# Masks on quarter tiles, K in four loads, early zero products and two tiles' K from memory, in a fused attention and mixture kernel

## The chip, the cores and the metric

The kernel runs on one core of a Trainium2 chip. The metric is the device time in microseconds of one execution. A profiled execution has a time of its own and a span, from its first to its last instruction. The engines are TensorE (PE, with its weight loads as PEld), VectorE (DVE), ScalarE (ACT), GpSimd (POOL) and SyncE (SP), whose queue issues all loads and stores here.

## What is computed

The reference chains three blocks. An attention with a window of 16 positions to each side and 24 block summaries, for 2 batches of 8 heads with 768 positions of 64 numbers; a feed-forward block with a Mish-like gate; a soft mixture of 8 experts with 4 slots each. Cut to what matters here:

```python
k_sum = k.reshape(B, H, nb, block, D).max(axis=3)
scores_l = scale * np.matmul(q, k.transpose(0, 1, 3, 2))
mask_l = np.abs(pos[:, None] - pos[None, :]) < window
scores_s = scale * np.einsum('bhsd,bhnd->bhsn', q, k_sum) + np.log(block)
scores_all = np.concatenate([np.where(mask_l, scores_l, -1e9), scores_s], axis=-1)
a = softmax(scores_all)
x = np.matmul(a, np.concatenate([v, v_sum], axis=2))   # 1536 tokens of 512
h = x @ w_in                                          # 512 to 2048
g = h * np.tanh(np.log1p(np.exp(h)))
x = g @ w_out                                         # then the soft mixture of experts
```

## The kernel before, in words

The 1536 tokens are 12 tiles of 128, six for each batch. Attention of a tile `t` handles two windows of 64 queries, with 96 neighbouring keys and 24 summaries each (KW = 120 columns). Its score step (`S`, L410 to L420) is 32 products on quarters of the PE array (64 rows by 64 columns, `tile_position`), four heads' pairs into two banks of 480 columns. For the first five tiles the mask is added by PE: a product of `spread_sb` (an identity over both halves, and three rows of ones) with a block of `mask_sb`, started ahead of the scores in the same bank (L414). It has the mask's 96 columns in rows 0 to 63 and the summand log(32) in rows 64 to 66 of columns 96 to 119. Later tiles get the mask on VectorE from a block made once (`near_mask`, `edge_mask`).

K of the first batch is loaded whole (`ld_kb`, L314, two loads of 768 KB), VectorE takes the block maxima (`ksum`, L319), and GpSimd copies the summaries (`kplace`, L372) and each tile's window (`windows`, L360) into the tile's K block. Tiles 0 to 5 all take their windows from there; tiles 8 to 11 load theirs from memory (`ld_k`, L401). After the scores come the row maximum (`red`, L427), its negative (`neg`, L431), exponentials on ScalarE (`exp`, L441), the reciprocal of the sums (`rc`), the scaling (`nm`, L456, on GpSimd or VectorE), the transposes (`AT`, L462) and the product with V (`AV`, L472).

Beside this the weights are prepared: `w_in` comes packed in eight loads (`ld_wi`, L496) through three staging slots, and each is decoded by ScalarE (`dec_a`, L487) and VectorE (`dec_s`, L488; `dec_o`, L489), which frees its slot for the next load. A scale per block is found (`gram`, `sc_bt`), and two half-precision planes are made (`wi_hi`, `wi_lo`, L519). Tile 0 goes through the first feed-forward product in full precision (`H32`, L611), later tiles by three plane products each (`H`, L617 to L619). `w_out` follows in the same way (`ld_wo`), with a folded matrix from it (`W2mm`, L570). Then each tile is routed (`route`), and the experts' weights stream in through whatever slots are free.

Every piece of work is a task. `ORDER` lists all 1281 of them in the order in which they are written to their engines' queues, `CHOICE` gives the engine of those that may run on several, and `SLOT` the buffer of each. So an engine does its tasks in the order of that table, and waits where one's inputs are late. The DMA queue has eight completion lanes: the ninth load of the program waits for the first to have landed, the tenth for the second, and so on.

## Time and profile before

| | us |
|---|---|
| median of 3 runs (lowest, highest) | 290.21 (289.18, 291.86) |
| profiled execution, its own time | 289.33 |
| its span | 287.5 |
| outside the span | 1.83 |
| busy in the span: PE, DVE, ACT, POOL | 268.0, 195.0, 207.8, 52.2 |

Busy times of PE are modelled ends, so a stretch that shows PE fully busy can hold slow products too. The granted clock is a share of PE's full rate (2.4 GHz), 0.5 of it being 1.2 GHz.

### The profile page before, as it was taken

The numbers are of one execution on the slowest core, as the hardware profiler recorded it, in microseconds if no ns is written. First come the engines' busy times: TensorE is split into PE (matmuls) and PEld (weight loads), VectorE is DVE, ScalarE is ACT, GpSimd is POOL, SyncE is SP. The second block draws the span as 40 slices with busy tenths as digits, with TensorE's granted clock in tenths as the row PEclk, the third lists the DMA queues.
The fourth block names the chain that finished last, engine by engine and source line by source line (L and its number), as shares of the span: only waits on it lengthen the run. The fifth ranks groups of instructions, "written<-read, shape, count | busy, mean of one in ns | idle before, by whom it ended". The sixth has DMA issues, their size and how long they took to land.

```text
span 287.5 us, 7828 instructions
## 1 busy us (share of the span) xinstructions
PE 268.0 (93%) x3144; PEld 151.4 (53%) x3144; DVE 195.0 (68%) x460; ACT 207.8 (72%) x488; POOL 52.2 (18%) x91
## 2 busy tenths in 40 slices
PE   0889879999999999999999999999999998999997
PEld 0557445555456564565556545455645743234475
DVE  2489899999999898778659667686523575002352
ACT  1297889979988879999969999899459653003232
POOL 1559225430070531001211111000000010100000
PEclk9997999999999999999999999999999999999999
DMA  7999999599999879999695677989988999999997
GB/s 253 415 358 344 358 339 365 137 335 308 317 246 315 154 107 222 205 241 223 241 192 128 76 222 141 299 157 210 325 317 313 370 388 314 412 423 421 423 346 252
DMA packets 58467, 80.58 MB, mean 280 GB/s; under 512 B 44352, under 2 KB 47936, under 8 KB 53824
## 3 DMA queue, kind: packets, MB, share of 16 engines
q1 hardware_dynamic: 58432, 80.10, 91.3%
q8 instruction: 24, 0.39, 0.5%
q14 instruction: 11, 0.09, 0.1%
HBM read 66.46 MB, written 3.15 MB: 242 GB/s over the span
## 4 chain that ended last, share of the span: by engine, by line
PE 44%; DVE 20%; DMA 16%; ACT 14%; issue 5%; POOL 1%; SPq 0%; DVEq 0%; ACTq 0%; POOLq 0%
PE bank L617 8%; PE bank L619 7%; PE bank L618 7%; DMA slot<-w2b 6%; DVE slot L489 4%; ACT slot L441 4%; DMA slot<-w2a 3%; PE bank L754 2%; ACT slot L625 2%; DMA slot<-kb 2%; DMA slot<-wi 2%; PE bank L472 2%; DVE slot L488 2%; DMA slot<-wo 2%; ACT L625 2%
## 5 line engine op out<-in xcount | busy, mean ns | idle before, releaser
L617 PE MATMUL bank<-slot,slot 128*128 128x512 f16 x176 | 66.9, 380 | 0.7 <-ACT slot L625 0.7
L618 PE MATMUL bank<-slot,slot 128*128 128x512 f16 x176 | 66.7, 379 | 0.0
L619 PE MATMUL bank<-slot,slot 128*128 128x512 f16 x176 | 66.7, 379 | 0.0
L456 POOL TENSOR_TENSOR slot<-slot,sm 128x480 f32<-128x480 f32 x19 | 22.7, 1197 | 91.7 <-DVE sm L452 25.2
L625 ACT ACTIVATE slot<-bank,scal 128x512 f32<-128x512 f32 x44 | 29.2, 687 | 9.8 <-PE bank L619 6.7
L641 DVE SCALAR_TENSOR_TENSOR slot<-slot,sc,slot 128x512 f16<-128x512 f32 x40 | 30.6, 774 | 4.3 <-ACT slot L637 4.0
L619 PEld LDWEIGHTS <-slot 128*128 128x128 f16 x176 | 17.2, 98 | 21.0 <-DVE slot L480 0.3
L255 ACT COPY slot<-bank 120x512 f32<-120x512 f32 (+5 forms) x45 | 17.7, 430 | 14.3 <-PE bank L923 8.3
L617 PEld LDWEIGHTS <-slot 128*128 128x128 f16 x176 | 17.4, 99 | 16.8 <-issue 0.6
L625 ACT ACT_TABLE_LOAD x20 | 25.7, 1283 | 0.8 <-PE bank L619 0.4
L618 PEld LDWEIGHTS <-slot 128*128 128x128 f16 x176 | 17.2, 98 | 16.6 <-issue 1.5
L441 ACT ACTIVATE slot<-slot,sm 128x120 f32<-128x120 f32 x56 | 21.3, 383 | 0.6 <-DVE sm L435 0.5
L441 ACT ACTIVATE slot<-bank,sm 128x120 f32<-128x120 f32 x40 | 13.9, 369 | 10.5 <-POOL sm L431 10.5
L257 DVE COPY slot<-bank 128x256 f32<-128x256 f32 (+3 forms) x30 | 14.4, 513 | 9.8 <-PE bank L462 4.0
L489 DVE SCALAR_TENSOR_TENSOR slot<-slot,slot 128x1024 int32<-128x1024 int32 x16 | 20.4, 1277 | 0.3
L487 ACT ACTIVATE slot<-slot 128x1024 f32<-128x1024 f32 x16 | 18.6, 1172 | 1.8 <-DMA slot<-wi 1.4
L462 PE MATMUL bank<-ident_sb,slot 128*120 128x128 f32 x96 | 14.7, 278 | 2.1 <-POOL slot L456 1.3
L360 POOL COPY slot<-slot 128x192 f32<-128x192 f32 x26 | 13.8, 550 | 12.4 <-DMA slot<-kb 12.3
L967 PE MATMUL bank<-slot,slot 128*32 128x384 f32 (+1 forms) x256 | 15.2, 382 | 0.2 <-DMA slot<-w2b 0.2
L611 PE MATMUL bank<-slot,slot 128*128 128x512 f32 x32 | 15.4, 599 | 0.0
L472 PE MATMUL bank<-slot,slot 120*64 120x64 f32 x384 | 14.6, 233 | 0.5 <-ACT phi_sb L385 0.3
L419 PE MATMUL bank<-slot,slot 64*64 64x120 f32 x384 | 14.2, 289 | 0.6 <-POOL slot L372 0.6
(175 smaller groups left out, 478.4 us busy)
## 6 DMA issues: line engine op xcount, KB each, us to landing
slot<-w SPq DMA_DIRECT2D x16, 1024.0 KB, 5.5
slot<-w2a SPq DMA_DIRECT2D x12, 960.0 KB, 9.0
slot<-wi SPq DMA_DIRECT2D x8, 1024.0 KB, 6.8
slot<-wo SPq DMA_DIRECT2D x8, 1024.0 KB, 6.0
slot<-vh SPq DMA_DIRECT2D x12, 384.0 KB, 5.3
slot<-w2b SPq DMA_DIRECT2D x4, 1024.0 KB, 18.6
slot<-kb SPq DMA_DIRECT2D x4, 768.0 KB, 5.5
slot<-qh SPq DMA_DIRECT2D x12, 256.0 KB, 5.4
```

The source lines that it names most:

```text
L255: sca.copy(dst, src)
L441: sca.activation(A_b[ha.slot][:, hp], src, AF.Exp, bias=m[:, hp:hp + 1], scale=1.0 if late else 0.125, accum_out=m[:, 4 + hp:5 + hp])
L456: (pool if e == "POOL" else vec).tensor_tensor(A_b[ha.slot], A_b[ha.slot], sm_t[hq.slot][:, 4:8].unsqueeze(2).to_broadcast([128, 4, KW]), ...
L472: pe.matmul(banks[hm.slot][64 * r:64 * r + 64, 128 * hp + 64 * w:128 * hp + 64 * w + 64], Vb[i][:, w, c:c + 64], AT_b[hat2[r].slot][0:KW, ...
L487: d = add("ACT", ("dec_a%d" % n,) + name, lambda e: sca.activation(dst(), st(1).bitcast(F32), AF.Prelu, scale=2.0 ** -112, alpha=-(2.0 ** ...
L489: return add("DVE", ("dec_o%d" % n,) + name, lambda e: vec.scalar_tensor_tensor(di(), st(0), 29, di(), op0=ALU.logical_shift_right, op1=AL ...
L611: pe.matmul(banks[hb.slot], xf_b(hx.slot)[:, dc], slots[hw.slot][:, 512 * dc:512 * dc + 512], start=(dc == 0), stop=(dc == 3))
L617: pe.matmul(ps, x[:, 0, dc], w[:, 0, dc], start=(dc == 0), stop=False)
L618: pe.matmul(ps, x[:, 0, dc], w[:, 1, dc], start=False, stop=False)
L619: pe.matmul(ps, x[:, 1, dc], w[:, 0, dc], start=False, stop=(dc == 3))
L625: g_done[t, fb] = [add("ACT", ("mish", t, fb), lambda e, dst=dst, hb=hb, sc=sc: sca.activation(dst(), banks[hb.slot], AF.Mish, scale=sc), ...
L641: d = add("DVE", ("glo", t, fb), lambda e: vec.scalar_tensor_tensor(pv(1), g(), sfb[:, t // TB:t // TB + 1], pv(0), op0=ALU.mult, op1=ALU. ...
```

## The change

- The mask products run on quarters of the array like the scores. `add_mask` writes the 96 mask columns and the 24 summand columns by two products of 64 rows by 64 columns each, once for each quarter, so eight small products stand where two (or, at an edge tile, four) stood. The constants are loaded so that both halves of the partitions hold them: `spread_sb`, `mask_sb` and the new `bias_sb` in two loads each. The two blocks made once for VectorE are built so as well.
- K of the first batch comes in four loads of 384 KB, each with its own block maximum. It lies in slots 4 and 5 rather than 6 and 7, and the full-precision blocks 2 and 3 of `w_in` move to slots 6 and 7.
- 22 products of zeros (`warm`, 128x128 by 480 columns) are added on PE, after GpSimd has zeroed `vsum`. They form a chain, and `vgather` of the first batch waits for the last.
- Tiles 4 and 5 load their K windows from memory, as tiles 8 to 11 do; eight window copies on GpSimd go.
- `ORDER`, `CHOICE` and `SLOT` are new as a whole (1309 tasks).

```diff
 ORDER = [
-    6, 7, 213, 11, 22, 189, 8, 12, 2, 192, 190, 3, 188, 191, 23, 25, 194, 195, 196, 197, 214, 0, 1, 215, 9, 10,
...
-    L_spread = add("DMA", ("ld_spread",), lambda e: dma(out=spread_sb, in_=spread))
-    L_mask = add("DMA", ("ld_mask",), lambda e: dma(out=mask_sb, in_=masks.rearrange("k p n -> p k n")))
+    for w in range(2):
+        L_spread = add("DMA", ("ld_spread", w), lambda e, w=w: dma(out=spread_sb[HALF[w]]..., in_=...), after=[L_spread])
+        L_mask = add("DMA", ("ld_mask", w), lambda e, w=w: dma(out=mask_sb[HALF[w]], in_=masks[:, 0:64].rearrange("k p n -> p k n")), after=[L_mask])
+        L_bias = add("DMA", ("ld_bias", w), lambda e, w=w: dma(out=bias_sb[HALF[w]], in_=masks[0, 64:128, 96:KW]), after=[L_mask])
...
+    def add_mask(ps, r, w, of, stop):
+
+        a, at = ps.shape[1], (64 * r, 64 * w)
+        for stat, mov, cols in ((slice(0, 64), mask_sb[HALF[r], of, 0:96], slice(0, 96)), (slice(64, 128), bias_sb[HALF[r]], slice(96, KW))):
+            pe.matmul(ps[HALF[w], :, cols], spread_sb[HALF[r], stat], mov.unsqueeze(1).to_broadcast([64, a, cols.stop - cols.start]), start=cols.start == 0, stop=stop and cols.start > 0, tile_position=at)
...
+    Z_w = add("POOL", ("fillw",), lambda e: pool.memset(vsum, 0.0))
+    for j in range(22):
+        warm.append(add("PE", ("warm", j), lambda e: pe.matmul(banks[hwarm.slot][:, 0:480], zeros[:, 0:128], zeros[:, 0:480], start=True, stop=True), [warm[-1]], ...))
...
+            for h in range(2):
+                k4.append(add("DMA", ("ld_kq", i, h), lambda e, i=i, h=h: dma(out=slots[hk[i].slot][:, 768 * h:768 * h + 768], in_=kb[b, :, 2 * i + h]), ...))
+                ks.append(add("DVE", ("ksumq", i, h), lambda e, i=i, h=h: vec.tensor_reduce(ksum[:, 2 * i + h], ..., op=ALU.max), [k4[-1]], use=[hk[i]]))
...
         if b == 0:
-            for t in range(2, TB):
-                K_in[t] = windows
+            K_in[2] = K_in[3] = windows
...
-                for rows, of in () if late else [(slice(0, 128), 1)] if kind == 1 else [(slice(0, 64), min(kind, 1)), (slice(64, 128), max(kind, 1))]:
-                    pe.matmul(ps[rows], spread_sb[:, rows], mask_sb[:, of].unsqueeze(1).to_broadcast([128, 4, KW]), start=True, stop=False)
+                for w, of in () if late else [(0, min(kind, 1)), (1, max(kind, 1))]:
+                    add_mask(ps, r, w, of, False)
```

SP's queue at the start, before: the two loads of K (`kb`) are the first, then the constants, one query tile (`qh`), and V's two (`vn`).

```order
L314 DMA slot_78<-kb 128x1536
L314 DMA slot_79<-kb 128x1536
L264 DMA spread_sb<-spread 128x128
L265 DMA mask_sb<-masks 128x3x120
L400 DMA slot_88<-qh 128x512
L262 DMA ident_sb<-ident 128x128
L263 DMA bmean_sb<-bmean 128x144
L316 DMA slot_87<-vn 128x1536
L316 DMA slot_95<-vn 128x1536
L400 DMA slot_89<-qh 128x512
L496 DMA slot_80<-wi 128x2048
```

The same place now.

```order
L268 DMA spread_sb<-spread 64x2x64 x2
L269 DMA mask_sb<-masks 64x3x120
L270 DMA bias_sb<-masks 64x24
L337 DMA slot_76<-kb 128x768 x2
L337 DMA slot_77<-kb 128x768 x2
L269 DMA mask_sb<-masks 64x3x120
L264 DMA ident_sb<-ident 128x128
L265 DMA bmean_sb<-bmean 128x144
L424 DMA slot_88<-qh 128x512
L270 DMA bias_sb<-masks 64x24
L424 DMA slot_89<-qh 128x512
L520 DMA slot_80<-wi 128x2048
```

Four small loads went ahead of K, the second halves of mask and summand stand behind it, and V's loads moved behind the first two of `w_in`.

PE between the first score step (its last row, L419 before) and the second one's masks, before: the edge block (L393) and the block means of V (L328) stand there.

```order
L419 MATMUL bank_65<-slot_90,slot_88 64x120 x2
L393 LDWEIGHTS spread_sb
L393 MATMUL bank_67<-mask_sb,spread_sb 64x120
...
L328 MATMUL bank_68<-slot_87,bmean_sb 24x128 x12
L328 MATMUL bank_68<-slot_95,bmean_sb 24x128 x12
L414 LDWEIGHTS spread_sb
L414 MATMUL bank_66<-mask_sb,spread_sb 128x480
```

The same place now; the pair of L290 stands there 14 times, and six more pairs stand ahead of the first score step.

```order
L443 MATMUL bank_65<-slot_90,slot_88 64x120 x2
L290 LDWEIGHTS vsum
L290 MATMUL bank_61<-vsum 128x480
...
L278 LDWEIGHTS spread_sb
L278 MATMUL bank_66<-mask_sb,spread_sb 64x4x96
L278 LDWEIGHTS spread_sb
L278 MATMUL bank_66<-bias_sb,spread_sb 64x4x24
```

Zero products took the place of the edge block and V's means, which now come after the second score step.

VectorE around the first decode of `w_in` (L488 and L489), before: its first half stands between the two maxima (L427) of tile 1, its second behind them and the scale of V.

```order
L456 TENSOR_TENSOR slot_91<-slot_91,sm_107 128x480
L427 TENSOR_REDUCE sm_108<-bank_66 128x4
L431 TENSOR_SCALAR sm_108<-sm_108 128x4
L488 TENSOR_SCALAR slot_77<-slot_77 128x1024
L427 TENSOR_REDUCE sm_109<-bank_64 128x4
L431 TENSOR_SCALAR sm_109<-sm_109 128x4
L302 TENSOR_REDUCE bnd<-bank_67 128x1
L287 TENSOR_REDUCE sm_110<-bnd 128x1
L489 SCALAR_TENSOR_TENSOR slot_77<-slot_80,slot_77 128x1024
```

The same place now (maxima L451, scaling L480, decode L512 and L513).

```order
L451 TENSOR_REDUCE sm_109<-bank_66 128x4
L480 TENSOR_TENSOR slot_91<-slot_91,sm_108 128x480
L451 TENSOR_REDUCE sm_110<-bank_64 128x4
L512 TENSOR_SCALAR slot_79<-slot_79 128x1024
L513 SCALAR_TENSOR_TENSOR slot_79<-slot_80,slot_79 128x1024
L475 TENSOR_SCALAR sm_109<-sm_109 128x4
L476 RECIPROCAL sm_109<-sm_109 128x4
```

Both halves of the decode now stand behind both maxima of tile 1, so behind the whole second score step.

## Rows read from the trace of the kernel before

**Rows 1.** The page: busy time, share of the span, instructions of each engine.

```profile
PE 268.0 (93%) x3144; PEld 151.4 (53%) x3144; DVE 195.0 (68%) x460; ACT 207.8 (72%) x488; POOL 52.2 (18%) x91
```

**Rows 2.** Windows: stretch, its length, busy times, granted clock, DMA share, GB/s.

```profile
core 0: us, PE busy (x) PEld busy (x) DVE busy (x) ACT busy (x) POOL busy (x), PEclk, DMA share, GB/s
5.00:10.00 5.00, 1.62 (x13) 0.92 (x17) 3.51 (x2) 0.00 (x0) 2.40 (x10) 1.00 1.07 394
...
50.00:55.00 5.00, 5.00 (x26) 2.02 (x25) 4.93 (x8) 5.00 (x13) 1.91 (x1) 1.00 0.72 184
...
60.00:287.50 227.50, 221.34 (x2646) 122.19 (x2644) 147.29 (x366) 164.39 (x384) 24.44 (x38) 1.00 0.92 269
```

**Rows 3.** Windows by stage, the same columns.

```profile
15.50:60.00 44.50, 39.56 (x399) 24.30 (x391) 42.59 (x89) 39.11 (x88) 21.75 (x28) 0.96 0.92 317
60.00:100.00 40.00, 39.36 (x468) 22.34 (x467) 38.61 (x70) 35.98 (x78) 10.03 (x18) 1.00 1.00 275
```

**Rows 4.** Timeline of SP's queue at the start: start, length, load [wait].

```profile
0.74 0.89 SPq L314 DMA_DIRECT2D slot<-kb  x2
1.67 0.42 SPq L264 DMA_DIRECT2D spread_sb<-spread  x1
2.14 0.56 SPq L265 DMA_DIRECT2D mask_sb<-masks  x1
...
4.31 1.29 SPq L316 DMA_DIRECT2D slot<-vn  x2
7.25 0.33 SPq L400 DMA_DIRECT2D slot<-qh  x1
```

**Rows 5.** Timeline of PE in the first score steps.

```profile
7.79 1.01 PE L414 MATMUL bank<-mask_sb,spread_sb 128*64 128x480 bf16 x4 [7.79 <-DMA mask_sb<-masks]
9.39 2.08 PE L419 MATMUL bank<-slot,slot 64*64 64x120 f32 x32 [0.59 <-POOL slot L372]
...
14.45 0.58 PE L414 MATMUL bank<-mask_sb,spread_sb 128*128 128x480 bf16 x2
14.96 1.05 PE L419 MATMUL bank<-slot,slot 64*64 64x120 f32 x32
...
20.90 1.63 PE L419 MATMUL bank<-slot,slot 64*64 64x120 f32 x32
```

**Rows 6.** Windows of one microsecond, the columns of rows 2.

```profile
22.00:23.00 1.00, 1.00 (x22) 0.70 (x16) 0.96 (x2) 0.96 (x6) 0.88 (x1) 0.50 0.94 328
```

**Rows 7.** Timeline of DVE to the end of the first decode.

```profile
7.26 1.75 DVE L319 TENSOR_REDUCE slot<-slot 128x48 f32<-128x1536 f32 x1 [0.22 <-DMA slot<-kb]
...
16.16 0.82 DVE L456 TENSOR_TENSOR slot<-slot,sm 128x480 f32<-128x480 f32 x1
...
16.90 0.64 DVE L427 TENSOR_REDUCE sm<-bank 128x4 f32<-128x480 f32 x1
...
17.66 0.69 DVE L488 TENSOR_SCALAR slot<-slot 128x1024 int32<-128x1024 int32 x1
...
19.71 1.31 DVE L489 SCALAR_TENSOR_TENSOR slot<-slot,slot 128x1024 int32<-128x1024 int32 x1
```

**Rows 8.** Timeline of PE: the fifth tile's step, the folded matrix, the end.

```profile
54.45 0.57 PE L414 MATMUL bank<-mask_sb,spread_sb 128*128 128x480 bf16 x2
...
61.83 1.08 PE L570 MATMUL bank<-slot,phi_sb 128*32 128x128 f32 x32 [0.21 <-DVE slot L489]
...
279.22 0.58 PE L664 MATMUL bank<-mask_sb,spread_sb 128*128 128x480 bf16 x2
...
282.75 3.20 PE L664 MATMUL bank<-mask_sb,spread_sb 128*128 128x480 bf16 x15
```

**Rows 9.** Groups by line on GpSimd: busy, mean ns, idle before.

```profile
L360 POOL COPY slot<-slot 128x192 f32<-128x192 f32 x26 | 13.8, 550 | 12.4 <-DMA slot<-kb 12.3
```

**Rows 10.** DMA issues: count, KB each, median us to landing.

```profile
out<-slot SPq DMA_DIRECT2D x3, 768.0 KB, 4.8
slot<-kh SPq DMA_DIRECT2D x4, 384.0 KB, 4.7
```

More of the change, by code (lines that the diff above doesn't have):

```diff
@@ L271, in const_fill @@
         pool.memset(bnd[:, 0:5], TINY2)
+    Z_w = add("POOL", ("fillw",), lambda e: pool.memset(vsum, 0.0))
+    hwarm = Hold(hring)
+    zeros = vsum.bitcast(BF16)
+    warm = [Z_w]
+    for j in range(22):
+        warm.append(add("PE", ("warm", j), lambda e: pe.matmul(banks[hwarm.slot][:, 0:480], zeros[:, 0:128], zeros[:, 0:480], start=True, stop=True), [warm[-1]], acq=[] if j else [hwarm], use=[hwarm] if j else []))
     Z_c = add("POOL", ("fill",), const_fill)
@@ L338, in batch @@
             V_read.extend([vs] + vm)
-        vc = add("ACT", ("vgather", b), gather, [vs] + old_v, use=[hb])
+        vc = add("ACT", ("vgather", b), gather, [vs] + (old_v or [warm[-1]]), use=[hb])
         if b == 0:
@@ L383, in near_mask, with mm @@
         hm = Hold(mring)
-        q = add("PE", ("near_mm",), lambda e: pe.matmul(banks[hm.slot][:, 0:KW], spread_sb, mask_sb[:, 1], start=True, stop=True), [L_spread, L_mask] + W2_parts, acq=[hm])
+        def mm(e):
+            for w in range(2):
+                add_mask(banks[hm.slot][:, 0:KW].rearrange("p (a k) -> p a k", a=1), 0, w, 1, True)
+        q = add("PE", ("near_m4",), mm, [L_spread, L_mask] + W2_parts, acq=[hm])
         near_done.append(add("ACT", ("near_ev",), lambda e: sca.mul(near, banks[hm.slot][:, 0:KW], 0.125), [q], use=[hm]))
@@ L391, in mm @@
             for n in range(2):
-                for rows, of in ((slice(0, 64), n), (slice(64, 128), n + 1)):
-                    pe.matmul(banks[hm.slot][rows, KW * n:KW * n + KW], spread_sb[:, rows], mask_sb[:, of], start=True, stop=True)
-        q = add("PE", ("edge_mm",), mm, [L_spread, L_mask], acq=[hm])
+                for w in range(2):
+                    add_mask(banks[hm.slot][:, KW * n:KW * n + KW].rearrange("p (a k) -> p a k", a=1), 0, w, n + w, True)
+        q = add("PE", ("edge_m4",), mm, [L_spread, L_mask], acq=[hm])
         edge_done.append(add("ACT", ("edge_ev",), lambda e: sca.mul(edge_t.rearrange("p n k -> p (n k)"), banks[hm.slot][:, 0:2 * KW], 0.125), [q], use=[hm]))
@@ L419, in sc @@
                         pe.matmul(banks[hs2[r].slot][64 * w:64 * w + 64, KW * hp:KW * hp + KW], Qb[i][d, 4 * w + hp], Kb[i][d, :, 4 * w + hp], start=late, stop=(late or hp == 3), tile_position=(64 * r, 64 * w))
[L420 removed]
+        s = add("PE", ("S" + ("" if late else "m4" if kind == 1 else "e4"), t), sc, [lq, *lks, kp[0], kp[1], L_spread, L_mask] + [last_S[0]], acq=hs2)
         last_S[0] = S_t[t] = s
```

30 lines of the change are left out of this document (18 added, 12 removed), and 160 rows, old and new, of tables (CHOICE, ORDER, SLOT).

## The prediction

> **What bounds the kernel now.** I read the busy shares first, then windows, then the timelines of the places that the change touches. PE is busy for 268.0 of 287.5 us [rows 1], so 19.5 us of idle time is all that a better order can win on PE, apart from slow products. By stage the idle time splits so: 8.4 us before 15.5 us (nearly all of it the wait for K and the masks), 4.9 between 15.5 and 60 (44.5 less 39.56), 6.2 after that (227.5 less 221.34) [rows 2, 3]. The reader is to see that the second part has another bound: VectorE is busy for 42.59 of 44.5 us there, and for 38.61 of 40 in the next stretch [rows 3]. It decodes and splits the weights and serves the softmax at once. Until 100 us VectorE has next to no slack, and from 60 us on PE has little either. So time lost at the start is not made up: whatever delays VectorE's first long stretch by one microsecond delays the whole by about one.
>
> The start itself: the first score step waits until 9.39 us, for K's summaries [rows 5], which come out of two block maxima of 1.75 us, the second from 7.26 on when K has landed [rows 7]. Its 32 products take 2.08 us, the second step's 1.05 [rows 5]: PE ran at half speed until about 14 us, though no window before 20 us shows a lowered clock. At 20.90 the same step takes 1.63 us, and there the granted clock does stand at 0.50, that is 1.2 GHz [rows 5, 6].
>
> **The start, part by part.** K now comes behind four small issues. An issue costs 0.42 (spread) to 0.56 us (masks) whole, and 0.33 is the shortest of these rows [rows 4]. Four make 1.3 to 1.9 us; I take 1.8, since a smaller load is not much cheaper to issue in these rows. So K's last quarter lands at 7.26 + 1.8 = 9.06. Its maximum is half of 1.75, 0.87, where the half K cost 1.75: ready at 9.93, and with 0.3 us for GpSimd's copies at 10.2, against 9.39. Behind K on the queue stand the second halves of mask and summand, with 0.45 MB of constants and queries between; at 394 GB/s [rows 2] these take 1.1 us, so they land at 10.2 as well. The summand's second half must also wait for the first quarter of K by the lanes, as the second V load (1.29 us for two issues) and the query load at 7.25 do now [rows 4]; that is over before it matters. Then come four of the mask products in front of the scores, some 0.4 us at half speed. The scores start at 10.6.
>
> Six zero products run ahead of that. A product of 480 columns takes 0.2 us at full speed (15 of them in 3.20, with the last one's end [rows 8]), so 0.4 at half: 2.4 us of work, over by 4 us, and then PE waits again until K is there. I therefore take the first step at half speed, as now: 10.6 + 2.08 = 12.7, where it ended at 11.47.
>
> Fourteen zero products follow before the second step. The speed rose at most 5.1 us after 9.39, when steady work began [rows 5]. From 10.6 that is 15.7: seven products at 0.4 (2.8, to 15.5) and seven at 0.2 (1.4), so the second step begins at 17.0. Its masks take 0.25 and its scores 0.98: it ends at 18.2, against 16.0 (14.96 + 1.05) [rows 5]. Before, the 2.98 us between the steps (11.47 to 14.45) were filled with work that had to be done at some time, V's means and the edge block; they now come later, at full speed.
>
> On VectorE the first decode ended at 21.02. It now stands behind the second step, a maximum (0.64), a scaling (0.82), another maximum, 0.69 and 1.31 [rows 7]: 4.1 us after 18.2 is 22.3, so +1.3. This first decode frees the staging slot that the fourth load of the weights waits for. From there to the folded matrix at 61.83 [rows 8] VectorE has the same set of tasks in both orders, in another sequence, and no room in either [rows 3]. **Start: +1.3 us**, between -1.3 (below, where the speed is up at the first step) and +4.0 (where the late loads and the late decode add).
>
> What the first of the Trainium skill's rules would make of this: TensorE: Matmul & The Clock Gate (Part 1, The HAM clock gate) says that the array starts throttled to half its clock and that sustained activity releases it. The slow first step agrees, 2.08 against 1.05 us; if six products were activity enough, the start would be the -1.3 of the rival below.
>
> **Masks.** A full step's two mask products take 0.51 us from their start to that of the scores [rows 5], 0.4 for the columns and 0.1 for the passage to quarter products. No row shows a mask on quarters. Below, four quarters run at once: 480 columns, 0.2 us. Above, one after the other: 0.8. The scores themselves are 32 quarter products in 1.0 us [rows 5], which fits four at a time, so I take 0.25. Only one step lies where PE is full, the fifth tile's at 54.45 [rows 8]: **-0.25** (bounds -0.3 and +0.3). In the second to fourth steps VectorE sets the pace, and the gain is hidden. The blocks made once for VectorE are under 0.5 us in all.
>
> A rule speaks against it: TensorEngine Tiling (Restrictions) has column tiling switch off the fast weight load, and every score step has eight such loads now. Its sum would be the upper bound, +0.3; no row shows a half-precision weight load of a quarter.
>
> **K of tiles 4 and 5.** Eight window copies of 0.55 us [rows 9] leave GpSimd, which is busy for 18% [rows 1]; PE's wait at the fourth tile went to a scaling, not to a copy, so I count nothing. Two loads of 384 KB are added, 4.7 us to landing each [rows 10]. They are issued ahead of the fifth and sixth tiles' score steps; between 50 and 55 us the queue moves 184 GB/s of the 394 it can [rows 2], and the fifth step comes at 54.45 [rows 8]. The cover is that lull; without it, 0.8 MB cost 2 us of the weight stream. **0** (0 to +2).
>
> **The rest.** After 62 us the work is the same, in another order. Idle time there is 6.2 us [rows 2]; I see no reason for less or more, so **0**, with 3, half of it, to either side. At the end the two filler products in front of the second output stage (0.58 [rows 8]) go, and a 768 KB store, 4.8 us to landing [rows 10], moves behind two small ones: 0 again (-0.6 to +1).
>
> Sum: +1.3 - 0.25 = +1.05 on 289.33, the profiled execution's time, gives 290.4. The median stands 0.88 above the profiled time, so **291.2 us**.
>
> **Rivals.**
> - *The speed is up at the first step.* The change does what its name says: the zero products before it suffice. Then the first step ends at 10.6 + 1.05 = 11.65, the fourteen take 2.8, the second step ends at 15.7 and the first decode at 19.8, 1.3 us earlier than now: 289.33 - 1.3 - 0.25 + 0.88 = 288.7. Against it: six products last 2.4 us and 6 us of waiting follow. Chance 0.2.
> - *The gaps close.* The new order has the planes of block 3 ready before the last decodes, and V's means and edge block as filler; it could use half of the 4.9 us of idle time up to 60 us and all of the 0.6 by which the step at 20.90 is slow: 289.33 - 2.5 - 0.6 - 0.25 + 0.88 = 286.9. Against it: VectorE is full there, and all of tile 0's products still stand ahead of tile 1's. Chance 0.13.
> - *The late loads and the late decode add.* The weights come in through three slots, so the stream is a loop: a decode frees a slot, a load fills it. If all of the 1.8 us that K costs the stream and the 2.2 us by which the second step is late come through, one at the load and one at the decode, the price is 4.0: 289.33 + 4.0 - 0.25 + 0.88 = 294.0. It decides from the point where the second `w_in` load lands later than its decode could start, that is if V's loads, now behind, don't give the time back. For it: VectorE has no slack. Against it: the first two weight loads move ahead of V's 1.5 MB, which is 4 us of the queue. Chance 0.2.
> - The forecast has 0.47.
>
> **The numbers.** About 1% (2.9 us) is what a measurement of this kernel can tell from no change. The forecast's own spread of some 2 us lies mostly within that; so does the first rival. Faster takes most of the second rival and a little of the spread below: 0.12. Slower takes most of the third and the forecast's upper end: 0.23. Same: 0.65. The range goes from the second rival's 286.9 to just over the third's 294.0, 294.4, with the 3 us of the rest inside it.
>
> **What would show it.** First scores at 10.6 and 2.1 us long; second step near 17; first decode's end near 22.3; the folded matrix's first product 1 to 2 us after 61.83; mask to scores 0.25 us at the fifth tile; idle time after 62 us near 6. The prediction is wrong if the first step runs at full speed, if VectorE shows gaps before 60 us (then the order and not the amount of work decides), or if the idle time after 62 us differs by over 3 us, which nothing in the profile of before can tell.

## The result, and the profile after

The changed kernel takes 292.49 us (median of 20 runs, 290.65 to 297.11) and the kernel before 290.75 (20 runs, 289.18 to 293.55). The ratio is 1.0058, with a 95% interval of 1.0035 to 1.0082: slower by 1.7 us, inside the 1% that was forecast as "same". A few executions fall in a slower state, over 1.5% above the fastest; the ratios, here and below, leave them out and compare with the kernel before as it ran beside each kernel (medians 290.13 to 290.82 in the experiments). The profiled execution took 293.19 us, its span 291.3.

The page's busy times of the changed kernel, which answer to [rows 1]:

```profile
PE 272.5 (94%) x3201; PEld 154.8 (53%) x3201; DVE 190.4 (65%) x455; ACT 207.1 (71%) x493; POOL 47.0 (16%) x80
```

PE is busy for 4.5 us more, though the work has not grown but for zero products and more, smaller mask products. Its windows, the columns of [rows 2, 3]:

```profile
5.00:10.00 5.00, 0.44 (x3) 0.01 (x1) 2.63 (x3) 0.00 (x0) 1.01 (x4) 1.00 0.98 339
15.50:60.00 44.50, 39.78 (x417) 24.96 (x416) 35.66 (x85) 36.21 (x95) 15.35 (x22) 0.92 0.92 320
60.00:100.00 40.00, 38.73 (x439) 21.86 (x437) 38.77 (x63) 36.48 (x62) 9.00 (x12) 1.00 1.00 301
60.00:291.30 231.30, 225.19 (x2737) 126.15 (x2734) 149.58 (x365) 169.26 (x398) 26.95 (x37) 1.00 0.92 273
```

The second line is the one to stop at: VectorE, busy for 42.59 of these 44.5 us before [rows 3], is busy for 35.66. In the changed kernel it waits there, 8.1 us in all, for PE (4.7) and for ScalarE (3.4), and ScalarE waits 3.7 us for loads of `w_in`. And PE's mean clock there is 0.92 instead of 0.96.

SP's queue at the start, against [rows 4]:

```profile
0.73 1.41 SPq L268 DMA_DIRECT2D spread_sb<-spread  x2
2.19 0.60 SPq L269 DMA_DIRECT2D mask_sb<-masks  x1
2.83 0.61 SPq L270 DMA_DIRECT2D bias_sb<-masks  x1
3.48 2.01 SPq L337 DMA_DIRECT2D slot<-kb  x4
...
7.78 0.49 SPq L270 DMA_DIRECT2D bias_sb<-masks  x1
8.30 0.58 SPq L424 DMA_DIRECT2D slot<-qh  x1
9.26 1.67 SPq L520 DMA_DIRECT2D slot<-wi  x2
```

K is issued 2.7 us later than before, and the first load of the weights (`slot<-wi`) at 9.26 us. PE in the first two score steps, against [rows 5], and at the fifth tile, against [rows 8]:

```profile
1.31 2.58 PE L290 MATMUL bank<-vsum 128*128 128x480 bf16 x6 [1.31 <-POOL vsum L285]
...
10.83 0.48 PE L278 MATMUL bank<-mask_sb,spread_sb 64*64 64x384 bf16 x1 [5.39 <-DMA mask_sb<-masks]
12.07 0.24 PE L278 MATMUL bank<-bias_sb,spread_sb 64*64 64x96 bf16 x1 [0.76 <-DMA bias_sb<-masks]
...
12.18 0.47 PE L443 MATMUL bank<-slot,slot 64*64 64x120 f32 x3
...
12.41 1.90 PE L443 MATMUL bank<-slot,slot 64*64 64x120 f32 x29
14.24 3.48 PE L290 MATMUL bank<-vsum 128*128 128x480 bf16 x14
17.66 0.37 PE L278 MATMUL bank<-mask_sb,spread_sb 64*64 64x384 bf16 x4
17.84 0.22 PE L278 MATMUL bank<-bias_sb,spread_sb 64*64 64x96 bf16 x4
17.88 1.02 PE L443 MATMUL bank<-slot,slot 64*64 64x120 f32 x32
...
62.15 0.37 PE L278 MATMUL bank<-mask_sb,spread_sb 64*64 64x384 bf16 x4
62.33 0.22 PE L278 MATMUL bank<-bias_sb,spread_sb 64*64 64x96 bf16 x4
62.37 1.01 PE L443 MATMUL bank<-slot,slot 64*64 64x120 f32 x32
```

The reader is to see three things. PE waits 5.39 us behind its six zero products and the first masks, and the first step still runs at half speed (2.13 us). The fourteen zero products take 3.48 us. And from the first mask product to the scores it is 0.22 us (17.66 to 17.88, 62.15 to 62.37) where it was 0.51.

VectorE's first decode ends at 22.78, where it ended at 21.02 [rows 7]:

```profile
20.64 0.68 DVE L512 TENSOR_SCALAR slot<-slot 128x1024 int32<-128x1024 int32 x1
21.36 1.42 DVE L513 SCALAR_TENSOR_TENSOR slot<-slot,slot 128x1024 int32<-128x1024 int32 x1
```

What PE waits for in all, how often, and the longest of each:

```profile
PE bank L278 <- DMA mask_sb<-masks: 5.9, 2, 5.4
PE bank L635 <- ACT slot L649: 2.1, 1, 2.1
PE bank L496 <- DMA slot<-vh: 1.4, 1, 1.4
PE bank L290 <- POOL vsum L285: 1.3, 1, 1.3
PE bank L443 <- DMA slot<-kh: 1.0, 1, 1.0
```

All but the first are new. The one at L635 is ScalarE, which stood behind the decode of the last load of `w_in`, and that decode waited for the load:

```profile
45.78 1.13 ACT L511 ACTIVATE slot<-slot 128x1024 f32<-128x1024 f32 x1 [2.61 <-DMA slot<-wi]
```

Before, this decode began at 42.06. At the end the third large store (L1028) is issued among the small ones (L1026), where the kernel before had issued all three large ones by 279.3 us and the first small one at 281.2:

```profile
278.63 1.89 SPq L1028 DMA_DIRECT2D out<-slot  x2
283.31 0.89 SPq L1026 DMA_DIRECT2D out<-slot  x2
284.30 0.67 SPq L1028 DMA_DIRECT2D out<-slot  x1
285.06 3.19 SPq L1026 DMA_DIRECT2D out<-slot  x4
```

To say where the time went I use four marks that every kernel here has: the first product of the half-precision planes (L617 before, L641 after), the first of the experts (L915, L939), the first of the second output stage (L987, L1011) and the span's end. Ahead of the first mark stand the same products in both kernels, but for masks and zeros.

| stretch | before | changed | difference |
|---|---|---|---|
| to the first plane product | 50.56 | 56.87 | +6.3 |
| from there to the first expert product | 193.27 | 190.39 | -2.9 |
| from there to the end | 43.67 | 44.04 | +0.4 |

The clock has to be read with care here. The trace's entries of the granted clock begin at 14.39 us before and at 15.24 in the changed kernel, each at 1.00. Ahead of the first entry a window shows 1.00 only because nothing is recorded, while the first score step takes 2.08 and 2.13 us where the same 32 products take 1.02 to 1.05 later. Behind it, and ahead of the first mark, 0.50 is recorded from 21.21 to 24.63 us before, and from 28.89 to 32.30 and from 49.37 to 52.78 in the changed kernel. The one stretch more is worth up to 1.7 of the 6.3 us. Of the -2.9 us, PE's idle time has 1.46 (4.90 to 3.44) and the shorter masks at the fifth tile 0.3; the rest is busy time that no run traces to an edit.

Single executions differ by much at the first mark: e11 below, the same program as before up to 270 us, reaches it at 53.16, 2.6 us after the profile of before. So the +6.3 is no measure of the change, and the profiled pair's 3.8 us is more than the medians' 1.7. The middle stretch is steadier: 193.05 to 193.76 us in the four profiles of the old order (before, e3, e10, e11), 189.77 to 191.33 in the ten of the new.

### The profile page after: what moved, and what is told of

It reads as the page before. It is cut to its first block, busy times and chain, and to the rows that moved or that the text cites. A ratio compares the mean times of both kernels' runs of the same rounds, so it can differ in the third digit from the quotient of the medians.

```text
span 291.3 us, 7927 instructions
## 1 busy us (share of the span) xinstructions
PE 272.5 (94%) x3201; PEld 154.8 (53%) x3201; DVE 190.4 (65%) x455; ACT 207.1 (71%) x493; POOL 47.0 (16%) x80
## 5 line engine op out<-in xcount | busy, mean ns | idle before, releaser
L641 PE MATMUL bank<-slot,slot 128*128 128x512 f16 x176 | 66.8, 380 | 0.0
L480 POOL TENSOR_TENSOR slot<-slot,sm 128x480 f32<-128x480 f32 x18 | 21.9, 1222 | 116.0 <-DVE sm L476 89.1
L649 ACT ACTIVATE slot<-bank,scal 128x512 f32<-128x512 f32 x44 | 29.8, 685 | 10.7 <-PE bank L643 9.0
L257 ACT COPY slot<-bank 128x256 f32<-128x256 f32 (+5 forms) x49 | 19.6, 429 | 21.8 <-PE bank L947 13.7
L665 DVE SCALAR_TENSOR_TENSOR slot<-slot,sc,slot 128x512 f16<-128x512 f32 x40 | 29.9, 756 | 2.8 <-DMA gx_t<-slot 2.4
L641 PEld LDWEIGHTS <-slot 128*128 128x128 f16 x176 | 17.3, 98 | 17.3 <-issue 0.8
L259 DVE COPY slot<-bank 128x256 f32<-128x256 f32 (+4 forms) x26 | 13.4, 519 | 14.0 <-ACT slot L257 8.2
L513 DVE SCALAR_TENSOR_TENSOR slot<-slot,slot 128x1024 int32<-128x1024 int32 x16 | 19.7, 1233 | 0.1
L635 PE MATMUL bank<-slot,slot 128*128 128x512 f32 x32 | 17.0, 662 | 2.1 <-ACT slot L649 2.1
L496 PEld LDWEIGHTS bank<-slot,slot 120*64 120x64 f32 x384 | 12.7, 142 | 4.2 <-issue 2.4
L486 PEld LDWEIGHTS bank<-ident_sb,slot 128*120 128x120 f32 x96 | 11.4, 141 | 5.9 <-issue 1.1
```

Source lines behind the costliest of these rows:

```text
L257: sca.copy(dst, src)
L480: (pool if e == "POOL" else vec).tensor_tensor(A_b[ha.slot], A_b[ha.slot], sm_t[hq.slot][:, 4:8].unsqueeze(2).to_broadcast([128, 4, KW]), ...
L486: pe.transpose(banks[ht.slot][0:KW, 128 * hp:128 * hp + 128], A_b[ha.slot][:, hp], ident_sb)
L496: pe.matmul(banks[hm.slot][64 * r:64 * r + 64, 128 * hp + 64 * w:128 * hp + 64 * w + 64], Vb[i][:, w, c:c + 64], AT_b[hat2[r].slot][0:KW, ...
L513: return add("DVE", ("dec_o%d" % n,) + name, lambda e: vec.scalar_tensor_tensor(di(), st(0), 29, di(), op0=ALU.logical_shift_right, op1=AL ...
L641: pe.matmul(ps, x[:, 0, dc], w[:, 0, dc], start=(dc == 0), stop=False)
```

## The experiments

Task numbers in the changed kernel: 35, 37, 40, 42 are K's loads, 2 and 5 spread, 3 and 6 the mask, 4 and 7 the summand, 222 the first query, 0 and 1 identity and block means. The theory after the result was that the stream of loads at the start passes its delay on; the rivals were the zero products, K of tiles 4 and 5, and the new order as such. All runs, with the marks of their profiles in us:

| run | median | ratio (95%) | first scores | first decode ends | last decode of `w_in` starts | first plane product | first expert product | second output stage | span |
|---|---|---|---|---|---|---|---|---|---|
| before | 290.75 | - | 9.39 | 21.02 | 42.06 | 50.56 | 243.83 | 279.79 | 287.5 |
| changed | 292.49 | 1.0058 (1.0035, 1.0082) | 12.18 | 22.78 | 45.78 | 56.87 | 247.26 | 281.87 | 291.3 |
| e1 K first | 291.86 | 1.0035 (0.9999, 1.007) | 12.01 | 23.48 | 44.52 | 54.55 | 244.49 | 280.36 | 290.2 |
| e2 six zeros | 292.10 | 1.0048 (1.0015, 1.008) | 12.37 | 22.76 | 46.76 | 56.44 | 247.22 | 281.40 | 291.6 |
| e3 before, small loads first | 291.54 | 1.0043 (1.0013, 1.0072) | 11.29 | 22.91 | 44.47 | 53.60 | 246.65 | 283.29 | 291.1 |
| e4 K of 4, 5 a quarter | 292.30 | 1.0068 (1.003, 1.0105) | 12.16 | 22.90 | 45.04 | 54.93 | 246.26 | 281.88 | 291.0 |
| e5 K and query first | 291.92 | 1.0046 (1.0009, 1.0083) | 10.02 | 21.72 | 44.80 | 54.67 | 244.44 | 280.54 | 290.0 |
| e6 old end | 293.34 | 1.0115 (1.0064, 1.0165) | 13.62 | 24.27 | 47.25 | 58.26 | 249.47 | 285.79 | 294.2 |
| e7 e5 and e6 | 290.86 | 1.0012 (0.9981, 1.0042) | 9.45 | 19.91 | 45.81 | 56.82 | 246.97 | 283.73 | 291.7 |
| e8 e7, six zeros | 291.22 | 1.0010 (0.997, 1.0049) | 10.02 | 20.42 | 43.36 | 53.34 | 243.21 | 279.25 | 287.5 |
| e9 small loads from ScalarE | 290.51 | 1.0025 (0.9991, 1.006) | 10.31 | 20.76 | 44.36 | 54.31 | 245.09 | 279.52 | 289.1 |
| e10 before, 29 zeros | 294.28 | 1.0125 (1.0079, 1.0172) | 9.84 | 22.02 | 44.96 | 54.30 | 248.06 | 284.41 | 293.0 |
| e11 before, late end | 292.13 | 1.0072 (1.0034, 1.011) | 9.40 | 21.03 | 44.84 | 53.16 | 246.92 | 282.14 | 291.2 |
| e12 start, end and zeros undone | 290.56 | 0.9995 (0.996, 1.0029) | 10.17 | 20.42 | 45.47 | 55.32 | 245.57 | 281.61 | 289.8 |

**e1: K first.**

```diff
+FIRST = [35, 37, 40, 42, 2, 5, 3, 4, 6, 7]
+ORDER = FIRST + [n for n in ORDER if n not in FIRST]
```

> The changed kernel with K's four loads issued first, and the six small loads of spread, mask and summand right behind them. In the changed kernel the data queue moved 24 GB/s in the first 5 us against 199 before, K's last quarter was landed at 10.6 us against 7.3, and the first scores began at 12.18 against 9.39. Theory 1 (the input stream is the bound of the first 50 us, so what it loses at the start comes through): K lands near 8, the scores begin near 10.3, the first plane product (56.87 us, before 50.56) comes some 2 us earlier, and the time falls by about 2 us, to a ratio near 0.999 of the kernel before. Theory 2 (the fourteen zero products and PE's order set the start): the first scores are earlier, the second step not by as much, the time falls by under 0.5 us, ratio 1.004 to 1.006. Theory 3 (the late order decides, not the start): no change of the time at all, 1.006.

K landed at 8.62 us, but the first scores came at 12.01, held by the first query load, which landed at 11.87. The second and third steps were even later, and yet the first plane product came 2.3 us earlier. The median fell by 0.6 us, which the interval does not separate from nothing, and not by theory 1's 2 us. The 2.3 us at the first plane product are no sign of a better start either: this profile has no stretch at 0.50 ahead of it, where the changed kernel's has two, 3.4 us of gain at most.

**e2: six zero products.**

```diff
-lambda e: pe.matmul(banks[hwarm.slot][:, 0:480], zeros[:, 0:128], zeros[:, 0:480], ...)
+lambda e, n=480 if j < 6 else 8: pe.matmul(banks[hwarm.slot][:, 0:n], zeros[:, 0:128], zeros[:, 0:n], ...)
```

> The changed kernel with the zero products from the seventh on cut from 480 columns to 8, so that they keep their places but take no time. Theory 2 (they stand in the way): the second step's masks come at 14.4 instead of 17.66 us, the first decode ends 1 to 2 us before 22.78, and the time falls by 1 to 2 us, to a ratio of 1.000 to 1.003. Theory 1 (the input stream is the bound): the second step is earlier, VectorE and ScalarE then wait for the weights instead, and the time stays within 0.5 us of the changed kernel's, ratio 1.004 to 1.007. A third way: without them PE stays at half speed until after the second step, which then takes 2.1 us instead of 1.0, and the time rises by 1 us, ratio near 1.009.

The second step began at 17.01 instead of 17.88, held now by its other inputs, and the first decode ended at 22.76, as in the changed kernel. The 3.48 us of zero products cover a wait that is there anyway. Theory 1's reading holds, 1.0048 lying in its band. The third way happened too: the second step ran at half speed, 2.1 us from 17.01 on.

```profile
17.01 0.47 PE L443 MATMUL bank<-slot,slot 64*64 64x120 f32 x2
17.24 1.90 PE L443 MATMUL bank<-slot,slot 64*64 64x120 f32 x30
```

So the fourteen do buy the speed of the second step, 1.02 us in the changed kernel, and that speed is not worth anything that can be seen in the time.

**e3: the kernel before with its small loads ahead of K** (0 and 1 are identity and block means there, 2 and 3 spread and mask).

```diff
+FIRST = [2, 3, 0, 1]
+ORDER = FIRST + [n for n in ORDER if n not in FIRST]
```

> The kernel before with its four small loads (spread, mask, identity, block means) issued ahead of K's two, and nothing else changed: K is issued some 2 us later. Theory 1 (what the start loses comes through, since K and then the weights are a stream without a gap): the first scores begin near 11.4 instead of 9.39 us and the time rises by 1.5 to 2.2 us, ratio 1.005 to 1.0075, which is the whole of the change's loss. Theory 3 (the start has slack behind it, and the late order decides): the first scores are as late, but the time rises by under 0.6 us, ratio 1.000 to 1.002.

The first scores were at 11.29, the first decode 1.9 us late, and the ratio 1.0043 is 1.25 us (0.4 to 2.1). Nothing else was changed, so a late start alone costs, in the kernel before, most of the 1.7 us that the change lost, as far as the interval tells. Theory 1 is right on the sign and a little high on the size; theory 3's band is left, though the interval touches it.

**e4: less of K from memory.** Only the first quarter of the columns is loaded for tiles 4 and 5.

```diff
-lambda e: dma(out=Kb[i][:, 0:4], in_=kh[t])
+lambda e, n=1 if t in (4, 5) else 4: dma(out=Kb[i][:, 0:n], in_=kh[t][:, 0:n])
```

> The changed kernel with the loads of K for tiles 4 and 5 cut to the first quarter of the columns (96 KB instead of 384 KB each; the other three quarters of these two tiles' K are what lay there, so their attention is not computed from the right K). If K from memory costs stream time: 0.58 MB less at 394 GB/s is 1.5 us, and the fifth score step's wait of 1.0 us for its K goes; the time falls by 1 to 2 us, ratio 1.000 to 1.003. If the loads are hidden, as the prediction counted: the wait of 1.0 us goes but the time stays within 0.4 us, ratio 1.005 to 1.007.

PE's wait of 1.0 us for `kh` was gone and the time stayed: 292.30 against 292.49, with intervals of about 1 us to either side. Within that the loads are hidden, as forecast.

**e5: K and the first query first**, as e1 with 222 behind 42.

> The changed kernel with K's four loads and the first query load issued first, and spread, mask and summand right behind. With K first alone the first scores still began at 12.01 us, since the first query load landed only at 11.87; yet the first plane product came at 54.55 against 56.87. If the first score step matters for what follows: the scores begin near 10.2, the first decode ends 1.5 us earlier than 22.77, the first plane product comes near 53.5, and the time is 1 to 1.5 us below the changed kernel's, ratio 1.000 to 1.003. If only the weights' loads matter: the first plane product stays near 54.5 and the ratio near 1.0035, as with K first alone. If the time is lost at the end (the last output products take 1.6 to 2.3 us longer there in all four runs of the new order), an early start gives 0.5 us at most, ratio 1.003 to 1.005.

The scores began at 10.02 and the first decode ended at 21.72, but the first plane product stayed where e1 had it (54.67, 54.55) and so did the time. So 2 us won on the first score step were worth nothing that can be seen. The loads show why. The columns of [rows 2], with GB/s last, for the kernel before, the changed one, and e5 twice:

```profile
0.00:12.50 12.50, 4.12 (x56) 2.87 (x60) 4.50 (x4) 1.28 (x1) 3.11 (x18) 1.00 0.88 319
0.00:12.50 12.50, 4.52 (x21) 1.71 (x24) 3.80 (x4) 1.28 (x1) 3.47 (x17) 1.00 0.69 224
0.00:12.50 12.50, 5.68 (x48) 3.31 (x49) 4.39 (x5) 1.28 (x1) 3.87 (x18) 1.00 0.70 223
7.50:12.50 5.00, 3.10 (x42) 2.58 (x43) 1.53 (x2) 0.00 (x0) 2.02 (x8) 1.00 0.62 182
```

By 12.5 us the queue has moved 4.0 MB before, 2.8 in the changed kernel and 2.8 in e5. With K first the hole in the stream is only moved: the small loads behind K wait for lanes, the first load of `w_in` is issued at 9.72 (9.26 in the changed kernel), and between 7.5 and 12.5 us the queue moves 182 GB/s. The fourth load of `w_in` lands at 30.65 us, as in the changed kernel (30.60), though the first decode ended 1.1 us earlier.

**e6: the old end on the changed kernel.** Tasks 1256, 1258, 1260 and 1263 are evictions and the first large store of the first output stage, 1273 to 1281 its last four products, their evictions and the third large store; 1287 is the third last product of the second weight stage, 1059 and 1079 are fillers. A buffer is taken from those free where the planned one is not.

```diff
+TAIL = [1260, 1256, 1258, 1263, 1275, 1276, 1277, 1278, 1273, 1274, 1279, 1280, 1281]
+ORDER = [n for n in ORDER if n not in TAIL]
+ORDER[ORDER.index(1287):ORDER.index(1287)] = TAIL
+END = [1059, 1079]
+ORDER = [n for n in ORDER if n not in END] + END
...
-                    h.slot = SLOT[h.n]
+                    h.slot = SLOT[h.n] if SLOT[h.n] in h.ring.free else min(h.ring.free)
```

> The changed kernel with the last products of the first output stage, their evictions and the third large store put back ahead of the last three products of the second stage, as the kernel before has them, and the two filler products that stood between output products put at the very end. From the first product of the second output stage to the end the kernel before took 7.75 us, the changed one 9.40. Theory of the end (the third 768 KB store is issued at 284.3 us, and the last small stores stand behind it): that stretch falls to 7.7 to 8.2 us and the time by 1.2 to 1.7 us, ratio 1.000 to 1.002. If the end waits for the last weights to land anyway, as the prediction's zero for the end says: the products of the second stage move later by as much as the first stage's take, and the time stays within 0.4 us, ratio 1.0045 to 1.007.

The stretch from the second output stage to the end did fall (294.20 - 285.79 = 8.4 us against 9.4), but the products moved ahead made the one from the first expert product to there longer (36.3 against 34.6). The time itself, six executions, lies above both bands (its interval, from 1.0064 on, touches the second); in the profiled one K's last quarter landed at 12.05 instead of 10.59 us, far ahead of the edit, and the delay was still there at the first plane product. This run says nothing for certain on the end.

**e7: e5 and e6 together.**

> Both of these together, the early start and the old end. If start and end are each a part of the loss and add: 2 to 3 us below the changed kernel, ratio 0.996 to 0.999, which is faster than both kernels. If they are one loss (what comes earlier into the last stretch waits there for the last 1 MB loads of the weights): no better than the end alone, ratio 1.000 to 1.002.

290.86 us, ratio 1.0012: level with the kernel before, not faster. Against e5 the stretch from the first expert product to the end is 0.8 us shorter (45.56 to 44.73), but three profiles with the end of before differ by more among themselves (43.67 before, 44.45 in e3, 44.94 in e10). The intervals of e5 and e7 overlap, so that start and end add is not shown.

**e8: e7 with six zero products.**

> The same with the zero products from the seventh on cut from 480 columns to 8. In the run with six zero products the second score step began 0.9 us earlier and the first decode ended at the same 22.76 us, so they should cost nothing: within 0.5 us of the run with start and end. If they cost what stands between the two steps (3.5 us of PE) once the first step is early, the time falls by 1 us or more against that run; if they buy the clock, it rises.

Within 0.4 us of e7: the fourteen cost nothing that can be seen, whether the first step is early or not. The second step took 2.13 us here, at half speed, against 1.01 in e7.

**e9: the small loads from ScalarE**, on top of e5's order (with 0 and 1 behind 7).

```diff
-    dma = nc.sync.dma_start
+    dma, dma_act = nc.sync.dma_start, nc.scalar.dma_start
...
-    L_ident = add("DMA", ("ld_ident",), lambda e: dma(out=ident_sb, in_=ident))
+    L_ident = add("DMA", ("ld_ident",), lambda e: dma_act(out=ident_sb, in_=ident))
...
```

> The changed kernel with K and the first query load issued first on SyncE, and the eight small loads (spread, mask, summand, identity, block means) issued from ScalarE, which has no work before 15 us. In the changed kernel the small loads cost SyncE 0.6 to 0.7 us each, and the first load of the weights was issued at 9.26 us against 7.62. If the small issues and their places in the eight lanes are what the start lost: the first load of the weights is issued near 4 us and lands near 13 instead of 15.1, the first scores begin near 10, the first plane product comes near 53 instead of 56.87, and the time is 2 to 2.5 us below the changed kernel's, ratio 0.997 to 1.000. If the rest of the new order holds it (the fourth load of the weights waits for the first decode in any case): as with K and the query first, ratio 1.002 to 1.005.

SyncE's queue in e9:

```profile
0.74 3.79 SPq L339 DMA_DIRECT2D slot<-kb  x4
6.01 1.61 SPq L426 DMA_DIRECT2D slot<-qh  x2
7.72 0.84 SPq L522 DMA_DIRECT2D slot<-wi  x2
```

The first load of the weights was issued at 7.72, not near 4: K's fourth load and the queries waited, with no small issue in front of them on this queue. The eight lanes are shared by both queues and the small loads hold five of the first eight. By 12.5 us the queue had moved 3.2 MB, and the fourth load of `w_in` landed at 30.38. The time came down to 290.51 us, in the second band, whose interval (0.9991 to 1.006) takes in both kernels. The Trainium skill, DMA: Bandwidth & Descriptors (Issuing engines are not separate DMA queues), says that issuing from several engines saves only the sequencer's time; the trace agrees: the first load of the weights was issued 1.5 us earlier (9.26 to 7.72) and landed 1.0 us earlier (15.13 to 14.13).

**e10: the kernel before with 29 zero products** ahead of the first step.

```diff
+ZEROS = list(range(1281, 1311))
+ORDER = ZEROS[:1] + ORDER
+ORDER[ORDER.index(194):ORDER.index(194)] = ZEROS[1:]
...
+    for j in range(29):
+        last = add("PE", ("warm", j), lambda e: pe.matmul(banks[hwarm.slot][:, 0:480], zeros[:, 0:128], zeros[:, 0:480], ...
```

> The kernel before with 29 zero products ahead of the first score step, enough to keep PE busy until K's summaries are there, and nothing else changed. This is the rival by which the speed is up at the first step, and in this run PE has no pause before it. If it holds: the 32 products of the first step take 1.05 us instead of 2.09, the second step begins at 14 instead of 14.96, the first decode ends 1 us before 21.02, and the time falls by about 1 us, ratio 0.996 to 0.998. If a start that is earlier on PE is not worth anything, because the weights' loads set the pace: the first step is short, the first plane product stays at 50.5 and the ratio is 0.999 to 1.001. If the products cost the clock later (the granted clock falls to 0.50 for some 2 us in many executions of these kernels): slower, ratio 1.002 to 1.006.

PE in e10, and its windows:

```profile
1.31 8.07 PE L1013 MATMUL bank<-vsum 128*128 128x480 bf16 x29 [1.31 <-POOL bnd L273]
...
9.84 1.05 PE L422 MATMUL bank<-slot,slot 64*64 64x120 f32 x32
...
14.07 1.05 PE L422 MATMUL bank<-slot,slot 64*64 64x120 f32 x32
...
20.31 1.11 PE L465 MATMUL bank<-ident_sb,slot 128*120 128x128 f32 x4 [3.17 <-ACT slot L258]
...
22.65 1.88 PE L422 MATMUL bank<-slot,slot 64*64 64x120 f32 x32
```

```profile
16.00:18.00 2.00, 1.14 (x20) 0.96 (x17) 1.14 (x3) 0.56 (x1) 0.00 (x0) 1.00 1.00 416
18.00:20.00 2.00, 0.00 (x0) 0.00 (x0) 1.37 (x3) 1.92 (x6) 0.23 (x1) 0.78 1.04 281
20.00:22.00 2.00, 1.63 (x6) 1.16 (x7) 1.97 (x5) 2.00 (x11) 2.00 (x3) 0.50 1.02 383
22.00:24.00 2.00, 2.00 (x30) 1.35 (x32) 1.66 (x8) 2.00 (x8) 1.38 (x2) 0.50 0.69 162
```

The first step takes 1.05 us and the second begins at 14.07: the mechanism of my first rival exists once PE has no pause. But PE then stands for 3.17 us until ScalarE has its copy, the granted clock falls to 0.50 during that wait, and it stays there to 26 us. On ScalarE the copy stands behind the first decode, which began at 17.44 instead of 15.84, since the first load of `w_in` had landed 1.6 us later (17.42 against 15.81); why it did is open. All six executions have a mean clock below 1.00. The time rises by 1.25%, more than the third band allows. The clock alone does not account for it: 0.50 is recorded for 10.2 us here and for 3.4 before, which is worth 3.4 of the profiles' 5.5 us at most. That sustained work raises the clock is also what the Trainium skill states in TensorE: Matmul & The Clock Gate (Part 1, The HAM clock gate); here the first step agrees, 1.05 us against 2.08 [rows 5].

**e11: the kernel before with the late end.**

```diff
+LATE = [1245, 1246, 1251, 1252, 1253]
+ORDER = [n for n in ORDER if n not in LATE]
+ORDER[ORDER.index(1280) + 1:ORDER.index(1280) + 1] = LATE
```

> The kernel before with two of its first-stage output products, their evictions and the third large store put behind the first products of the second output stage, as the changed kernel has them. Theory of the end (the order there costs 1 to 1.6 us): from the first product of the second output stage to the end it takes 9 to 9.4 us instead of 7.75, and the time rises by 1 to 1.5 us, ratio 1.003 to 1.005. If the last weights' landing sets the end, or what is moved behind the second stage's first products takes its time from ahead of them: the time stays within 0.4 us, ratio 0.9985 to 1.0015.

From the second output stage to the end it took 9.1 us (291.2 - 282.14) instead of 7.7, as the theory of the end has it; from the first expert product to the end 44.3 instead of 43.7. But 2.6 us of this profile's 3.7 were there at the first plane product, 220 us ahead of the edit. And 44.3 from the first expert product lies between e3's 44.45 and the 43.67 of before, whose ends are the same. The time did rise, the interval being clear of 1, but the ratio of 1.0072 can't be put down to the end.

**e12: start, end and zero products undone**: e9, the end of e6, and all zero products cut to 8 columns. K in four loads, the masks, K of tiles 4 and 5 and the rest of the new order stay.

> The changed kernel with the small loads issued from ScalarE, K and the first query first, the old order at the end, and all 22 zero products cut from 480 columns to 8. The zero products have now been seen to cost clock: with 29 of them ahead of the first step the step ran in 1.05 us, but the granted clock stood at 0.50 from 19 to 26 and again at 43 to 47 us, and the time rose by 1.2%. If the losses of the start, of the end and of the zero products are separate and add: 1 to 1.5 us below the run with the small loads on ScalarE (290.51 us), ratio 0.997 to 1.000, level with the kernel before or just below it. If the early start is already all that can be had (the last stretch waits for the last weights, which land some 18 us after their issue): the same as that run, ratio 1.001 to 1.004.

290.56 us, ratio 0.9995: the loss is gone, and nothing is won; the interval (0.996 to 1.0029) lies below that of the changed kernel. Which of the three edits did it, the runs don't separate. The second step now ran at half speed (2.13 us from 14.68) and the first decode still ended at 20.42, as in e8.

## Why the prediction was right, and where it was not

The forecast, 291.2 us and "same", held, and the range held 292.49. That it came so near is in part luck: as far as one pair of profiles tells, the changed kernel is 6.3 us later at the first plane product, where 1.3 less 0.25 was forecast, and gains 2.9 in the middle, where nothing was. By its steps:

- *K behind four small issues, +1.8.* It is 2.7 at issue: the four small issues ahead of it cost 0.60 to 0.70 us each, more than the 0.42 and 0.56 of whole tiles [rows 4] from which I took my bounds. K's last quarter landed at 10.6, not 9.06, the second half of the mask with it, at 10.8, and that of the summand at 12.0, where 10.2 was forecast for both. The first step waited for that one: it came at 12.2, not 10.6, and was about 2.1 us long as forecast.
- *Fourteen zero products, second step at 17.0, first decode at 22.3.* 17.88 and 22.78. The fourteen took 3.48 us and not 4.2, since the clock rose 3.1 us after the first scores and not 5.1. The start's term of +1.3 is what e3 measured for a late start alone on the kernel before (1.25 us, 0.4 to 2.1).
- *"Time lost at the start is not made up", since VectorE has no slack until 100 us.* This step failed in its reason. VectorE was busy for 35.66 of 44.5 us, and waited for engines that waited for loads. e5 won 2 us on the first step and 1 us on the first decode, and nothing of it shows in the time. In the five profiles of the new order with no 0.50 recorded ahead of the first plane product (e1, e4, e8, e9, e12) the first decode ends between 20.42 and 23.48 us and that product comes between 53.34 and 55.32, in no order with it: the two with 20.42 have the earliest and the latest. A late start does cost time in the kernel before (e3), but in the new order it is not VectorE's lateness that comes through. The stream of loads is late there, as the table below shows; ahead of the fourth load of `w_in` it carries the same data in both kernels, with V's now behind the first two. Then 1.7 to 4.0 us come back before the experts, in every profile of the new order.
- *Masks, -0.25.* 0.22 us instead of 0.51: -0.29. The upper bound, +0.3, which was also what I made of the Trainium skill's rule in TensorEngine Tiling (Array Packing), Restrictions, is not what the trace shows: a weight load of a quarter takes 104 ns on average at the fifth tile, one of the whole array took 98.
- *K of tiles 4 and 5, 0.* e4 shows no cost, to within 1 us.
- *The rest, 0, idle time after 62 us near 6.* Idle is 6.1 us (231.3 less 225.19 from 60 us on), but this stretch now holds more of the work, so the agreement says little; measured from mark to mark the middle gained 2.9 us, at the edge of the 3 that I allowed.
- *The end, 0 (-0.6 to +1).* The stretch from the second output stage is 1.7 us longer (9.4 against 7.7), but the one ahead of it is shorter; from the first expert product on it is +0.4 in the changed kernel and +0.6 in e11, less than the 1.3 by which profiles with the same end differ (43.67, 44.45, 44.94). So nothing contradicts the 0, and no run shows a loss at the end that is clear of that spread.

The rivals: the speed was not up at the first step, and e10 shows that it would have gained nothing in this form. Of the second (the gaps close), the third step did run in 1.02 instead of 1.63 us, but PE's idle time from 15.5 to 60 us stayed (4.72 against 4.94); the gaps that closed lie behind, in the middle.

Of the third (late loads and late decode), the late loads are at work, and the late decode is not. At the second load of the weights its condition was not met (landed at 17.61, decoded from 21.63). At the fourth it looks met: issued at 22.84 when the first decode freed its slot, landed at 30.60, against 21.09 and 26.75 before. But the runs with an earlier decode answer this:

| run | first decode ends | third load of `w_in` lands | fourth is issued | fourth lands |
|---|---|---|---|---|
| before | 21.02 | 24.30 | 21.09 | 26.75 |
| e3 | 22.91 | 25.22 | 22.98 | 28.00 |
| e1 | 23.48 | 27.93 | 23.55 | 31.68 |
| changed | 22.78 | 26.80 | 22.84 | 30.60 |
| e5 | 21.72 | 26.82 | 21.79 | 30.65 |
| e9 | 20.76 | 26.63 | 20.83 | 30.38 |
| e8 | 20.42 | 26.59 | 20.49 | 30.48 |
| e7 | 19.91 | 25.86 | 19.98 | 29.80 |

The fourth load follows the landing of the third and not its own issue: 3.75 to 4.03 us after it in nine of the ten profiles of the new order (4.9 in e6), 2.4 to 2.8 in the four of the old, while from its issue it takes 7.7 to 10.0 and 5.0 to 6.0 us. The stream is what is late: in the changed kernel the third load lands 2.5 us later than before, and tile 0's V, which lands between the two, at 28.40, landed at 22.08 before, ahead of the third.

What stays open: how the 1.7 us divide between start, end and zero products (e12 undoes all three at once; alone, in the changed kernel, none has an effect clear of noise), and what, edit by edit, makes the middle of the new order 1.7 to 4.0 us shorter. No run moves V's loads back ahead of the weights, so that they hold the fourth load is argued from the landings and not tested.

## What to carry to other kernels

An engine that is busy for 96% of a stretch is not yet its bound: ask whether it would still be full if its inputs came later. Then follow the stream of loads to the one that it ends up waiting for, and test a suspected release by a run in which it comes earlier: here the fourth load did not move. At the start of a program small loads cost issue time and lanes wherever they stand among the large ones: ahead of K they made K late, behind K they made a hole ahead of the weights. Making one engine faster ahead of a partner that has not changed can only move the wait, as in e10, where the clock fell within it. And before two profiles are compared stage by stage, look at how far two executions of one program lie apart there.

## What the runs showed of the hardware

- Spread, mask and summand, loaded by halves of the partitions, took SyncE 0.49 to 0.70 us each to issue (two of spread in 1.41), and ScalarE 0.52 to 0.69 (e9), where the whole spread and mask took 0.41 to 0.56 and a K load of 768 KB 0.45 [rows 4].
- The eight completion lanes hold for the loads of both queues together: in e9 SyncE issued K's fourth load, the ninth of both, at 4.20 us, right after the first had landed at 4.18.
- As far as the steps' times show, the trace's entries of the granted clock begin where the clock first rises. In e2 that is at 24.93 us, and the score step from 17.01 on takes 2.1 us, the one from 26.50 on 1.02; in e10 it is at 5.45, and the first step, from 9.84, takes 1.05. A mean clock counts what lies ahead as full: e8's profile has 1.00, though its first two steps take 2.13 us each.
- Executions of one kernel differ in TensorE's recorded clock: of 100 of the kernel before, run beside the experiments, 39 had a mean clock of 1.00 (median 289.9 us) and the rest less (291.0). The changed kernel had 1.00 in 16 of 20, with a median of 292.5. A mean of 1.00 says only that no fall was recorded, so what the change costs at equal clock is not shown.
